# Token-mixing weights fetched earlier, their copies spread over three slots, and one pair's k squares moved to GpSimd

## The chip, the cores and the metric

One core of a Trainium2 chip. The time is that of the device for one execution, in microseconds (us); medians are of the runs that one call made. A profile is one traced execution of the kernel. "Before" is the tuned kernel, "changed" is the one under study.

## The reference, cut to what matters

```python
def _attn_ref(q, k, v, tau):                    # 8 batches, 12 heads, 448 rows, 64 wide
    q_n = q / (np.linalg.norm(q, axis=-1, keepdims=True) + 1e-06)
    k_n = k / (np.linalg.norm(k, axis=-1, keepdims=True) + 1e-06)
    scores = np.matmul(q_n, k_n.transpose(0, 1, 3, 2)) / tau
    ...                                         # softmax
    return np.matmul(attn, v).astype(np.float32)

def _moe_ref(x, w_tok1, w_tok2, w_ch1, w_ch2):  # x is the attention output, 8 x 448 x 768
    xt = x.transpose(0, 2, 1)
    h = np.maximum(xt @ w_tok1, 0.0) @ w_tok2   # token mixing: the weights of this case
    u = x + h.transpose(0, 2, 1)
    h2 = np.maximum(u @ w_ch1, 0.0) @ w_ch2     # channel mixing: most of the matmuls
    return (u + h2).astype(np.float32)
```

## The kernel before

Two heads make a pair; 48 pairs run through a loop whose pass i is called slot i here. A slot computes the scores of pair i (psS, then psX for its 64 rest rows), their exponentials on ScalarE, and the products with v of pair i-1 (psO). Token mixing follows two and three slots later: psR multiplies with w1, its relu is r, psU multiplies with w2. Once six pairs are done, channel mixing (psG, psF) fills TensorE. q and k are normalised first: squares (GpSimd and ScalarE), sums (VectorE), a logarithm and exponential on ScalarE, the scaling on GpSimd, then transposes on TensorE and a copy on VectorE, the "qk copy". The instructions of each engine run in the order in which they are written.

```python
def weights_tok():                                  # all three fetches on GpSimd's queue
    nc.gpsimd.dma_start(out=w1t[:, 0:NC, :], in_=moe_w_tok1[0:SM]...)
    nc.gpsimd.dma_start(out=w1t[0:XR, NC, :], in_=moe_w_tok1[SM:S])
    w2n.append(mix.tile([P, TT, S], FP16, name="w2n", tag="gt16", bufs=1))
    nc.gpsimd.dma_start(out=w2n[0][:], in_=moe_w_tok2...)

def place_w2():                                     # big copy, then a small one
    nc.vector.tensor_copy(out=w2t[:, :, XR:S]..., in_=w2n[0][:, :, 0:SM]...)
    nc.vector.tensor_copy(out=w2t[:, :, S:S + XR], in_=w2n[0][:, :, SM:S])
def place_w2_odd():                                 # small copy for odd batches
    nc.vector.tensor_copy(out=w2t[:, :, 0:XR], in_=w2n[0][:, :, SM:S])

def scaled(p, eng):                                 # k, then q, times their norms
    ...
        eng.tensor_tensor(out=kqs[...], in0=src, in1=_bcast_free(rn, E), op=ALU.mult)
# ... the opening, pair 0 ...
weights_tok()
cast_vx(0)                                          # GpSimd: rest rows of v
cast_v(0)                                           # VectorE: v to 16 bits
scaled(2, nc.gpsimd)
for i in range(NP_ALL + 2):
    ...
    elif 0 < i < NP_ALL:
        score(i, 0, 2 if i < 4 else 0)              # two filler matmuls ahead
        score(i, 1)
        score(i, 2)
    ...                                             # sums, norms, squares, scaling
    if i <= FIRST:
        casts()                                     # cast_v(1) in slot 3
    if i < FIRST:
        for p in tok2_at.get(i, ()):
            tok2(p)                                 # psU
        if i == 3:
            next_qk(i + 1)                          # transposes and qk copy
        if i:
            pv(i - 1)
        if i:
            score_x(i)
        if i in (0, 1, 2, 4):
            next_qk(i + 1)
        for p in tok_at.get(i, ()):
            m_tok1(p)                               # psR and r
    ...
    if i == 2:
        place_w2()
    if i == 3:
        place_w2_odd()
```

Of the kernel before, what the change touches and what calls it, by code (L numbers as in the profile page):

```python
# [22 lines left out]
def kernel(  # L23
# [12 lines left out]
    nc = tc.nc  # L36
# [100 lines left out]
    def mh(at, p):  # L137
        return at[p // HP][:, 2 * (p % HP):2 * (p % HP) + 2]

    def weights_tok():  # L140
        nc.gpsimd.dma_start(out=w1t[:, 0:NC, :], in_=moe_w_tok1[0:SM].rearrange("(p c) t -> p c t", c=NC))
        nc.gpsimd.dma_start(out=w1t[0:XR, NC, :], in_=moe_w_tok1[SM:S])
        w2n.append(mix.tile([P, TT, S], FP16, name="w2n", tag="gt16", bufs=1))
        nc.gpsimd.dma_start(out=w2n[0][:], in_=moe_w_tok2.rearrange("(tt p) s -> p tt s", p=P))

    def place_w2():
        nc.vector.tensor_copy(out=w2t[:, :, XR:S].rearrange("t a (c p) -> t a c p", c=NC),
                              in_=w2n[0][:, :, 0:SM].rearrange("t a (p c) -> t a c p", c=NC))
        nc.vector.tensor_copy(out=w2t[:, :, S:S + XR], in_=w2n[0][:, :, SM:S])  # L149

    def place_w2_odd():
        nc.vector.tensor_copy(out=w2t[:, :, 0:XR], in_=w2n[0][:, :, SM:S])

    def weights_ch1(i):
        n = C // 2
# [31 lines left out]
    def squares_x(n, eq, ek):  # L187
        square(eq, sqx[0:XR, 0:6], xh(xq, n, 6))
        square(ek, sqx[:, 6:9], xh(xk, n, HP))
# [9 lines left out]
    def rnorms(n, c0=0, c1=45):  # L199
        ssq, rn = ssqs[n % 3][:, c0:c1], rns[n % 3][:, c0:c1]  # L200
        nc.scalar.activation(out=rn, in_=ssq, func=AF.Ln, bias=tiny[:])
        nc.scalar.activation(out=rn, in_=rn, func=AF.Exp, scale=0.5)
        nc.scalar.activation(out=rn, in_=rn, func=AF.Ln, bias=eps[:])  # L203
        nc.scalar.activation(out=rn, in_=rn, func=AF.Exp, scale=-1.0)  # L204
# [242 lines left out]
    def at(slots):  # L447
        got = {}
        for p, s in slots.items():
            got.setdefault(s, []).append(p)  # L450
        return got


    FIRST = NPAIR
    early_sq = {3: 0, 4: 1, 5: 1, 6: 3, 7: 4, 8: 5, 9: 5, 10: 6, 11: 7, 12: 8, 13: 9, 14: 9, 15: 10, 16: 11, 17: 11}
    sq_slot = {p: early_sq.get(p, p - 6) for p in range(3, NP_ALL)}
    sq_at = at(sq_slot)
    sum_at = at({p: s + 1 for p, s in sq_slot.items() if p < 8 or p >= 18})

    rn_at = {}  # L460
    for n in range(1, NHALF):
        for c0, c1 in ((0, 21), (21, 45)) if n < 4 else ((0, 45),):
            s = 1 + sq_slot[3 * n + (0 if c1 == 21 else 2)]
            rn_at.setdefault(s, []).append((n, c0, c1))
    sc_at = at({p: {7: 6}.get(p, p - 2 if p < DMA_FROM else p - 3) for p in range(3, NP_ALL)})
    early_qk = {2: 0, 3: 4, 4: 6, 5: 7}
# [45 lines left out]
    with tc.manual_schedule():  # L512
# [53 lines left out]
        tpose_main(0, pst, 0)  # L566
        tpose_main(0, pst, 1)
        squares_x(0, nc.scalar, nc.gpsimd)
        rnorms(0, 21, 33)
        scaled(1, nc.gpsimd)  # L570
        nc.scalar.copy(out=qks[0][:, 0:SM], in_=pst[:, 0:SM])
# [14 lines left out]
        rnorms(0, 33, 45)  # L586
        score_rest0()
        score_x(0)
        weights_tok()
        cast_vx(0)  # L590
        cast_v(0)
        scaled(2, nc.gpsimd)
        for i in range(NP_ALL + 2):
            if i < DMA_FROM:
                loads(i)
            if DMA_FROM <= i + 2 < NP_ALL:
                dma_tpose(i + 2)
            if i - 2 in X_DMA:
                x_tpose(i - 2)
            for p in ut_at.get(i, ()):  # L600
                u_tpose(p)
            if i >= DMA_FROM:
                loads(i)

            left = next((t + 1 - i for t in sorted(tok2_at) if t >= i + (i == FIRST) and
                         any(p % NPAIR == NPAIR - 1 for p in tok2_at[t])), 6)
            if FIRST <= i < 2 * NPAIR:
                quota = max(len(queue) - 6, 0) * ns(S, DT) / (2 * NPAIR - i)
            else:
                quota = max(sum(t for t, _ in queue) - 2000.0, 0.0) / left  # L610
            def next_qk(p):
                if p < min(DMA_FROM, NP_ALL):
                    qk_copy(p, tpose(p))

            def tok2(p):
                m_tok2(p)
                if p % NPAIR == NPAIR - 1:
                    queue.extend(ch_units(p // NPAIR))

            def norm_rn():  # L620
                for n, c0, c1 in rn_at.get(i, ()):
                    rnorms(n, c0, c1)

            def next_sq(ps):
                for p in ps:
                    norm_begin(p, nc.scalar if p < 18 else nc.gpsimd, nc.scalar if p == 3 else nc.vector if p in (10, 11, 12, 15) else nc.gpsimd)

            if i == FIRST:
                next_sq([9])
                rnorms(2, 21, 33)  # L630
                norm_scale(7, nc.gpsimd)
                pv(i - 1)
                m_tok1(i - 2)
                tok2(i - 3)
                next_qk(i)
                tok2(i - 2)
                m_tok1(i - 1)
                score(i, 0)
                score(i, 1)
                score(i, 2)  # L640
                tok2(i - 1)
                norm_sums(8)
                norm_sums(9)
            elif 0 < i < NP_ALL:
                score(i, 0, 2 if i < 4 else 0)
                score(i, 1)
                score(i, 2)
            for p in sum_at.get(i, ()):
                norm_sums(p)
            if i < FIRST:  # L650
                norm_rn()

            if i < FIRST:
                next_sq([p for p in sq_at.get(i, ()) if p != 9])
                for p in sc_at.get(i, ()):
                    norm_scale(p, nc.gpsimd)
            def casts():
                for n in castx_at.get(i, ()):
                    cast_vx(n)
                for n in cast_at.get(i, ()):  # L660
                    cast_v(n)
                if i in (2, 5):
                    weights_ch1(i // 4)
                if i in (7, 8):
                    weights_ch2(i - 7)

            if i <= FIRST:
                casts()

            if i < FIRST:  # L670
                for p in tok2_at.get(i, ()):
                    tok2(p)
# [9 lines that stand above are left out]
                    m_tok1(p)  # L682
            elif i == FIRST:
                feed(0.0, 1000.0)
                score_x(i)
                feed(0.0, 1000.0)
                rnorms(2, 33, 45)
                norm_scale(8, nc.gpsimd)
                rnorms(3, 0, 21)
                next_qk(i + 1)  # L690
                next_sq(sq_at[i])
                norm_sums(10)
                feed(0.0, 1000.0)
            else:
                def norm_next():
                    norm_rn()
                    for p in sc_at.get(i, ()):
                        norm_scale(p, nc.gpsimd)

                if i >= 2 * NPAIR:  # L700
                    next_sq(sq_at.get(i, ()))
                if i < DMA_FROM:
                    norm_next()
                    casts()
                fed[0] = 0.0
                feed(quota * 0.3, 900.0 if i < DMA_FROM else 1800.0)
                if i < NP_ALL:
                    score_x(i)
                if i >= DMA_FROM:
                    norm_next()  # L710
                    casts()
                next_qk(i + 1)
                if i <= NP_ALL:
                    pv(i - 1)
                both = [p for p in tok2_at.get(i, ()) if p in tok_at.get(i, ())]
                if not both:
                    feed(quota * 0.3)
                for p in tok_at.get(i, ()):
                    m_tok1(p)
                if i < 2 * NPAIR:  # L720
                    next_sq(sq_at[i])
                if both:
                    feed(quota * 0.3, 900.0)
                for p in tok2_at.get(i, ()):
                    tok2(p)
                if i < 2 * NPAIR:
                    for p in sq_at[i]:
                        norm_sums(p)
                feed(quota * 0.4, 900.0 if i >= 2 * NPAIR else 0.0)
            if i == 2:  # L730
                place_w2()
            if i == 3:
                place_w2_odd()
        for p in ut_at.get(NP_ALL + 2, ()):
            u_tpose(p)
        feed(1e9)
# [35 lines left out]
```

## Time and profile before

| | before |
|---|---|
| median of 3 runs | 393.95 us (393.75 to 393.95) |
| span of the profiled run | 391.6 us |
| TensorE busy | 378.7 us, 97% |
| first psU starts | 27.44 us, after 1.14 us of idle TensorE |
| first psG starts | 44.54 us |

The page's lines and the waits that bound it are in the prediction below. Two more views: what GpSimd and VectorE do around the first psU. The columns are start and duration in us, engine, line, operation, output<-input, shapes and count; in brackets, the idle time before and what ended it. First GpSimd, before:

```profile
25.40 0.83 POOL L211 TENSOR_TENSOR kq<-km,rn 128x384 f16<-128x384 f32 x1 [1.41 <-ACT rn L204]
26.19 1.14 POOL L211 TENSOR_TENSOR kq<-qm,rn 128x384 f16<-128x384 f32 x1
27.29 1.17 POOL L172 CAST vx<-xv 64x192 f16<-64x192 f32 x2
```

The first two lines are the scaling of pair 4's k and q (L211), the third the cast of v's rest rows. And VectorE, before:

```profile
25.56 1.09 DVE L147 COPY w2t<-w2n 128x768 f16<-128x768 f16 x1
26.57 0.81 DVE L149 COPY w2t<-w2n 128x128 f16<-128x128 f16 x1
27.31 0.93 DVE L166 CAST vt<-vm 128x1152 f16<-128x1152 f32 x1
...
31.00 0.49 DVE L152 COPY w2t<-w2n 128x128 f16<-128x128 f16 x1
```

These are the three w2 copies (L147, L149, L152) and the cast of v's second half (L166).

### The profile page before, as it was taken

How to read it: one execution, taken by the hardware profiler on the slowest of the kernel's cores; microseconds unless marked ns; L12 is line 12 of the kernel's file. 1: busy time of each engine (PE TensorE's matmuls, PEld its weight loads, DVE VectorE, ACT ScalarE, POOL GpSimd, SP SyncE). 2: the span in 40 equal slices, each digit the busy share in tenths (PEclk: the TensorE clock that was granted, in tenths of full speed). 3: DMA queues.
4: the chain of work that ended last, by engine and by line, in shares of the span. 5: the costliest groups of instructions: out<-in, count | busy, mean ns of one | idle time of the engine just before them, and what ended most of it. 6: DMA issues, size and time to landing. Idle time of an engine off the chain costs nothing.

```text
span 391.6 us, 9075 instructions
## 1 busy us (share of the span) xinstructions
PE 378.7 (97%) x3658; PEld 228.9 (58%) x3658; DVE 193.6 (49%) x368; ACT 226.1 (58%) x411; POOL 209.6 (54%) x306
## 2 busy tenths in 40 slices
PE   7678999999999999999999999999999999999996
PEld 2356655665565656565566565565566566565554
DVE  5688758866244654446534545346434342333022
ACT  5998698843765548673775546673765535511400
POOL 4978486589476675768673938658551700000000
PEclk9699999999999999999999999999999999999999
DMA  8999989988988988999999899799982453023013
GB/s 204 267 242 221 256 238 187 201 213 241 208 170 200 211 166 194 222 166 223 199 239 174 177 253 206 155 192 175 244 142 55 133 114 69 16 60 102 3 40 121
DMA packets 137514, 67.51 MB, mean 172 GB/s; under 512 B 93248, under 2 KB 134016, under 8 KB 137472
## 3 DMA queue, kind: packets, MB, share of 16 engines
q1 hardware_dynamic: 133296, 61.36, 72.0%
q0 software_dynamic: 3632, 5.18, 7.7%
q8 instruction: 28, 0.46, 0.5%
q10 hardware_dynamic: 544, 0.39, 0.3%
q14 instruction: 14, 0.11, 0.1%
HBM read 43.38 MB, written 11.01 MB: 139 GB/s over the span
## 4 chain that ended last, share of the span: by engine, by line
PE 88%; ACT 7%; DVE 3%; DMA 1%; issue 1%; SPq 0%; DVEq 0%
PE psF L404 28%; PE psG L389 28%; PE psO L320 9%; PE psS L301 7%; PE psR L341 5%; PE psU L361 4%; ACT pt L302 3%; PE psO L322 3%; PE psX L308 2%; DMA qm<-in_q_dram 1%; PE psU L366 1%; ACT sq L178 1%; PE pst L243 1%; ACT pt L309 1%; ACT rn L203 1%
## 5 line engine op out<-in xcount | busy, mean ns | idle before, releaser
L302 ACT ACTIVATE pt<-psS 128x896 f16<-128x896 f32 x141 | 119.1, 921 | 64.6 <-PE psS L301 64.3
L389 PE MATMUL psG<-ut,wc1t 128*128 128x448 f16 x576 | 119.5, 353 | 0.2
L404 PE MATMUL psF<-wc2t,gt 128*128 128x384 f16 (+2 forms) x684 | 117.3, 323 | 0.1
L391 ACT ACTIVATE gt<-psG 128x448 f16<-128x448 f32 x96 | 51.1, 557 | 71.9 <-PE psG L389 71.9
L404 PEld LDWEIGHTS <-gt 128*128 128x128 f16 x684 | 64.5, 98 | 47.1 <-issue 6.8
L389 PEld LDWEIGHTS <-wc1t 128*128 128x128 f16 x576 | 53.2, 98 | 52.4 <-issue 8.7
L211 POOL TENSOR_TENSOR kq<-km,rn 128x384 f16<-128x384 f32 x47 | 39.4, 838 | 77.4 <-ACT rn L204 77.2
L407 DVE TENSOR_TENSOR ost<-psF,ur 128x384 f32<-128x384 f32 (+2 forms) x57 | 31.4, 550 | 87.2 <-PE psF L404 87.2
L320 PEld LDWEIGHTS <-pt 128*128 128x128 f16 x1152 | 50.8, 98 | 8.5 <-issue 2.4
L320 PE MATMUL psO<-vt,pt 128*128 128x65 f16 x1152 | 53.1, 194 | 1.1 <-ACT pt L302 0.8
L326 DVE RECIPROCAL rec<-psO 128x8 f32<-128x8 f32 x48 | 9.9, 207 | 81.5 <-PE psO L322 81.5
L193 DVE TENSOR_REDUCE ssq<-sq 128x12 f32<-128x768 f32 (+1 forms) x49 | 45.1, 929 | 6.0 <-ACT sq L178 3.1
L180 POOL TENSOR_TENSOR sq<-km 128x384 f32<-128x384 f32 x42 | 34.4, 822 | 15.1 <-DMA km<-in_k_dram 14.8
L322 PE MATMUL psO<-vx,pt 128*128 128x130 f16 x192 | 42.1, 219 | 0.0
L211 POOL TENSOR_TENSOR kq<-qm,rn 128x384 f16<-128x384 f32 x47 | 39.6, 842 | 0.0
L301 PE MATMUL psS<-qk 64*128 64x448 f16 x282 | 36.2, 357 | 1.3 <-DVE qk L261 0.9
L327 DVE TENSOR_TENSOR x<-psO,rec 128x512 f16<-128x512 f32 x48 | 33.2, 691 | 1.7
L341 PE MATMUL psR<-x,w1t 128*128 128x128 f16 x384 | 29.2, 219 | 0.1
L309 ACT ACTIVATE pt<-psX 128x448 f16<-128x448 f32 x48 | 27.1, 564 | 3.3 <-PE psX L308 2.3
L361 PE MATMUL psU<-w2t,r 128*128 128x448 f16 x96 | 25.9, 353 | 1.5 <-DVE w2t L149 1.1
L180 POOL TENSOR_TENSOR sq<-qm 128x384 f32<-128x384 f32 x30 | 24.7, 823 | 1.1 <-DVE ssq L193 0.3
L341 PEld LDWEIGHTS <-w1t 128*128 128x128 f16 x384 | 23.8, 97 | 2.1 <-issue 0.4
(76 smaller groups left out, 320.4 us busy)
## 6 DMA issues: line engine op xcount, KB each, us to landing
vm<-in_v_dram SPq DMA_DIRECT2D x16, 576.0 KB, 5.3
out_dram<-ost SPq DMA_DIRECT2D x23, 384.0 KB, 2.9
qm<-in_q_dram SPq DMA_DIRECT2D x14, 576.0 KB, 5.2
km<-in_k_dram SPq DMA_DIRECT2D x14, 576.0 KB, 5.2
wc1t<-in_moe_w_ch_dram POOLq DMA_DIRECT2D x2, 1152.0 KB, 13.9
wc2t<-in_moe_w_ch_dram POOLq DMA_DIRECT2D x2, 1152.0 KB, 12.9
out_dram<-ost SPq DMA_DIRECT2D x9, 192.0 KB, 2.7
xq<-in_q_dram SPq DMA_DIRECT2D x7, 192.0 KB, 5.1
```

The lines of the kernel that those rows point to most:

```text
L180: eng.tensor_tensor(out=out, in0=src, in1=src, op=ALU.mult)
L193: nc.vector.tensor_reduce(out=ssqs[p // HP % 3][:, lo + 6 * a0:lo + 6 * a1], in_=sq[p][:, a0:a1].rearrange("p a g e -> p (a g) e"), axis=A ...
L211: eng.tensor_tensor(out=kqs[n % 2][:, j, a, 0:NC, :].rearrange("p c (g e) -> p g c e", g=2), in0=src, in1=_bcast_free(rn, E), op=ALU.mult)
L301: nc.tensor.matmul(psS[:, g, 0:S], qk[r, P * c:P * (c + 1)], qk[r, 512:512 + S], start=True, stop=True)
L302: nc.scalar.activation(out=pt[:, 2 * S * c:2 * S * (c + 1)].rearrange("p (g s) -> p g s", g=2), in_=psS[:, :, 0:S], func=AF.Exp, scale=inv ...
L320: nc.tensor.matmul(psO[:, m, E1 * g:E1 * (g + 1)], pt[:, at:at + P], vt[:, 2 * j + g, c, 0:E1], start=(g == 0 and c == 0), stop=False)
L322: nc.tensor.matmul(psO[:, m, 0:2 * E1], pt[:, PX + P * m:PX + P * (m + 1)], vx[:, j, 0:2 * E1], start=False, stop=True)
L341: nc.tensor.matmul(psR[:, tt, :], w1t[:, m, tt * P:(tt + 1) * P], xs[p][:, m, :], start=(m == 0), stop=(m == NC))
L361: nc.tensor.matmul(psU, rs[p][:, tt, :], w2t[:, tt, lo:lo + S], start=(tt == 0), stop=by_dma and tt == TT - 1)
L389: nc.tensor.matmul(psG[:], wc1t[:, dt, ct * P:(ct + 1) * P], ut[:, dt, sp], start=(dt == 0), stop=(dt == DT - 1))
L391: nc.scalar.activation(out=gt[:, ct, sp], in_=psG[:], func=AF.Relu)
L404: nc.tensor.matmul(psF[:, 0:w], gt[:, ct, lo:lo + P], wc2t[:, ct, P * i0:P * i1], start=(ct == 0), stop=(ct == CT - 1))
```

## The change

It means to have w2 in place before the first psU. (1) The main part of w1 is fetched ahead of pair 1's scaling, where GpSimd is idle, so that w2's fetch can be issued earlier. (2) The big w2 copy moves to the end of slot 1; the small ones stay at the ends of slots 2 and 3. (3) Pair 3's k squares, and those of the rest rows, go from ScalarE to GpSimd, ahead of pair 2's scaling.

```diff
+        weights_tok1(0)                 # main part of w1, in the opening
         rnorms(0, 21, 33)
         scaled(1, nc.gpsimd)
...
-        weights_tok()
+        weights_tok2()
+        weights_tok1(1)                 # rest rows of w1
         cast_vx(0)
         cast_v(0)
+        squares_x(1, nc.scalar, nc.gpsimd)
+        squares(3, nc.scalar, nc.gpsimd)
         scaled(2, nc.gpsimd)
...
+            if i == 1:
+                place_w2()              # now the big copy alone
             if i == 2:
-                place_w2()
+                place_w2_x(S)
             if i == 3:
-                place_w2_odd()
+                place_w2_x(0)
```

More of the change, by code (lines that the diff above doesn't have):

```diff
@@ L138, in mh, with weights_tok1, weights_tok2 @@
         return at[p // HP][:, 2 * (p % HP):2 * (p % HP) + 2]
-    def weights_tok():
-        nc.gpsimd.dma_start(out=w1t[:, 0:NC, :], in_=moe_w_tok1[0:SM].rearrange("(p c) t -> p c t", c=NC))
-        nc.gpsimd.dma_start(out=w1t[0:XR, NC, :], in_=moe_w_tok1[SM:S])
+    def weights_tok1(x):
+        if x:
+            nc.gpsimd.dma_start(out=w1t[0:XR, NC, :], in_=moe_w_tok1[SM:S])
+        else:
+            nc.gpsimd.dma_start(out=w1t[:, 0:NC, :], in_=moe_w_tok1[0:SM].rearrange("(p c) t -> p c t", c=NC))
+    def weights_tok2():
         w2n.append(mix.tile([P, TT, S], FP16, name="w2n", tag="gt16", bufs=1))
@@ L148, in place_w2, with place_w2_x @@
                               in_=w2n[0][:, :, 0:SM].rearrange("t a (p c) -> t a c p", c=NC))
-        nc.vector.tensor_copy(out=w2t[:, :, S:S + XR], in_=w2n[0][:, :, SM:S])
-    def place_w2_odd():
-        nc.vector.tensor_copy(out=w2t[:, :, 0:XR], in_=w2n[0][:, :, SM:S])
+    def place_w2_x(lo):
+        nc.vector.tensor_copy(out=w2t[:, :, lo:lo + XR], in_=w2n[0][:, :, SM:S])
     def weights_ch1(i):
@@ L454 @@
     FIRST = NPAIR
-    early_sq = {3: 0, 4: 1, 5: 1, 6: 3, 7: 4, 8: 5, 9: 5, 10: 6, 11: 7, 12: 8, 13: 9, 14: 9, 15: 10, 16: 11, 17: 11}
-    sq_slot = {p: early_sq.get(p, p - 6) for p in range(3, NP_ALL)}
+    early_sq = {4: 1, 5: 1, 6: 3, 7: 4, 8: 5, 9: 5, 10: 6, 11: 7, 12: 8, 13: 9, 14: 9, 15: 10, 16: 11, 17: 11}
+    sq_slot = {p: early_sq.get(p, p - 6) for p in range(4, NP_ALL)}
     sq_at = at(sq_slot)
-    sum_at = at({p: s + 1 for p, s in sq_slot.items() if p < 8 or p >= 18})
+    sum_at = at({p: s + 1 for p, s in ({3: 0} | sq_slot).items() if p < 8 or p >= 18})
     rn_at = {}
@@ L462 @@
         for c0, c1 in ((0, 21), (21, 45)) if n < 4 else ((0, 45),):
-            s = 1 + sq_slot[3 * n + (0 if c1 == 21 else 2)]
+            s = 1 + ({3: 0} | sq_slot)[3 * n + (0 if c1 == 21 else 2)]
             rn_at.setdefault(s, []).append((n, c0, c1))
@@ L625, in next_sq @@
                 for p in ps:
-                    norm_begin(p, nc.scalar if p < 18 else nc.gpsimd, nc.scalar if p == 3 else nc.vector if p in (10, 11, 12, 15) else nc.gpsimd)
+                    norm_begin(p, nc.scalar if p < 18 else nc.gpsimd, nc.vector if p in (10, 11, 12, 15) else nc.gpsimd)
             if i == FIRST:
```

## The prediction

> **What bounds the kernel now.** I read the page's busy table first, then the 40 slices, then the waits of TensorE, and last the order of time of each engine in the first 50 us.
>
> The busy table and the slices of the kernel before:
>
> ```profile
> PE 378.7 (97%) x3658; PEld 228.9 (58%) x3658; DVE 193.6 (49%) x368; ACT 226.1 (58%) x411; POOL 209.6 (54%) x306
> ...
> PE   7678999999999999999999999999999999999996
> ...
> PEclk9699999999999999999999999999999999999999
> ```
>
> From the fifth slice on (39 us) the PE row reads 9 to the end: nothing but fewer or shorter matmuls can shorten that part, and the change touches no matmul. What the change can touch lies before 45 us. There PE is idle 391.6 - 378.7 = 12.9 us in all, most of it early. The waits of TensorE over the whole run, those over 0.5 us:
>
> ```profile
> PE pst L247 <- DVE kq L222: 1.8, 1, 1.8
> PE busy L236 <- POOL id L543: 1.4, 1, 1.4
> PE psU L361 <- DVE w2t L149: 1.1, 1, 1.1
> PE psS L301 <- DVE qk L261: 0.9, 2, 0.6
> PE psS_r L288 <- DVE qk L585: 0.8, 1, 0.8
> PE psO L320 <- ACT pt L302: 0.8, 2, 0.5
> ```
>
> The first, second and fifth end before 13.7 us, in a part whose order on PE, DVE and ACT the change leaves alone. The third is what it aims at: the first token mixing (psU) waits for VectorE to lay out w2. The chain that ended last, followed in order of time, goes through the same place:
>
> ```profile
> 16.88 2.54 ACT pt L302 x3
> ...
> 24.75 0.56 DVE qk L261
> 25.31 0.33 DVE r L344
> 25.64 1.01 DVE w2t L147
> 26.65 0.75 DVE w2t L149
> 27.40 0.04 issue
> 27.44 0.54 PE psU L361 x2
> ```
>
> The reader is to see that the two w2 copies, 1.01 + 0.75 us, stand on the chain, between the token activation r and the matmul that uses it. PE had finished the scores of slot 3 at 26.30 us and stood still until 27.44.
>
> **What the Trainium skill says.**
> - "Perfetto Trace Analysis", Identifying the Most-Contended Engine and the strategy after it: matmul busy share is a poor distance to the roofline, and a kernel may have several regimes, whose gaps are to be read within each. The trace agrees on the second point: PE is idle 1.14 us of the 1.14 us at 26.30 to 27.44 and 3.55 of the 346 us after 45.
> - "SBUF — State Buffer", Who interferes with whom: a VectorE instruction with two SBUF inputs, or a copy in a two-port mode, and a GpSimd instruction block each other, whichever starts second waiting. The trace fits: the 128x128 w2 copy took 0.81 us at 26.57 and 0.49 us at 31.00, and GpSimd's scaling beside the first took 1.14 us where it usually takes 0.83.
> - "DMA: Bandwidth & Descriptors", Issuing engines are not separate DMA queues: a transfer issued by GpSimd shares the 16 engines with those of SyncE. The trace agrees as far as it goes: from 13 us the DMA row is full and SyncE's issues stretch to 2.75 and 3.67 us; from 9 to 11 us the share is only 0.70.
> - "TensorE: Matmul & The Clock Gate", What's actually happening: the clock is granted by recent activity, half of it when cold. In this trace the granted clock is 0.50 from about 12.6 to 19.4 us and 1.00 after.
>
> **The change, part by part.** Slot i is the loop's pass i; pair numbers are those of the scores.
>
> *1. Fetching w1 earlier.* The main w1 fetch (0.74 us of GpSimd to issue) moves from 12.71 us to about 7.47 us. There GpSimd had an idle stretch of 1.45 us before pair 1's scaling at 8.91 us, which waits for ScalarE's norms. 7.47 + 0.74 = 8.21, so it hides. The fetch of w2 then starts 14.35 - 12.71 = 1.6 us earlier; it took 7.2 us to land, so I expect it about 12.7 + 7.2 = 19.9 us, where it was 21.6. The transfer moves into the stretch where the DMA share was 0.70. w1 itself is first read at 24.42 us and had landed by about 20. Direct gain: none. It frees 0.74 us of GpSimd behind 12.7 us, and makes part 2 possible.
>
> *2. w2's copies apart.* The big one (L147) goes from the end of slot 2 to the end of slot 1. VectorE there: the qk copy of pair 2 ends about 21.12; then two reductions of 0.9 until 22.92; then idle 0.89 until 23.81, when pv(1) is done. With the copy: 21.12 + 1.01 = 22.13, + 1.80 = 23.93, so the reciprocal starts about 23.95, some 0.15 us late. That delay falls on the qk copy of pair 3 (ends 25.40 for 25.23) and on r. The scores of slot 3 start at 25.41 anyway, behind two filler matmuls, so they lose about 0.05. r ends about 25.71. One small copy (0.41 to 0.75) is left before psU: 26.1 to 26.5. PE is free at about 26.35. psU so starts at 26.35 to 26.5 and not at 27.44: 0.95 to 1.1 us gained. The third copy (L152) stays where it was.
>
> *3. Pair 3's k squares on GpSimd.* ScalarE loses two instructions, at 15.69 and 16.52: 0.42 + 0.36 = 0.78 us. But the exponentials that follow start at 16.88, and the first two score matmuls of slot 1 run from 16.28 at half clock and take 0.57, so end at 16.85. ScalarE becomes free at 16.1 and waits there: the gain is 0.02 us. GpSimd gains 0.82 + 0.50 = 1.32 us of squares and has lost 0.74 of issue, so pair 2's scaling ends about 17.55 + 0.6 = 18.1; its transposes start at 19.69. The reduction of pair 3 then starts about 16.5 and ends with the rest-row sums about 18.1, ahead of the norms at 19.29. GpSimd's pairs 4 and 5 squares end about 19.8, ahead of the scaling at 20.55, which waits for ScalarE.
>
> *Does the gain last until PE is the bound?* From psU on I move everything by 1.0 and look for what holds. ScalarE: exponentials of slot 3 at 25.86 + 2.41, two squares of 0.41, then psX's exponential at about 29.1 and not 30.01. It had been idle 0.87 there, so 0.9 is all that can pass. Scores of slot 4 about 29.7 (30.61). Pair 5's scaled k and q were ready on GpSimd at 32.20 and read at 33.20; GpSimd does not move by 1.0 but loses less to the copies (0.3 us), so 31.9 against a need at 32.3: it holds. wc1's first half landed at 28.39 + 14.0 = 42.4, read at 44.54: slack 2.1. The k of half 3 landed at 27.97 + 14.6 = 42.6 and its sums were read at 45.3 after another sum: slack about 1.4. So about 0.85 us should reach the stretch that is bound by PE, and stay. **Sum**: -1.0 at psU, +0.05 at the scores, +0.1 on ScalarE, -0.02 from part 3: -0.85 us, and 393.95 - 0.85 = 393.1 us.
>
> **The rivals.**
> *A: w2 lands late.* If it came at 22 us or later, the big copy would hold VectorE's queue, and with it the sums of pairs 4 and 5, pv(1) and the scores of slot 3; the wait would only have moved. For it: DMA is full from 13 us. Against it: 7.2 us to land, as measured, ends at 19.9, some 1.2 us before the copy. It would give 393.7 to 394.2.
> *B: GpSimd becomes the bound early.* Pair 3's scaling and rest rows end at 23.99 and their transpose runs at 24.14: no slack. The big copy at 21.1 now runs beside them, and may lengthen them by 0.3 us, as the copies lengthened pair 4's scaling. That would move the qk copy of pair 3, already 0.15 late, to 0.3 late. It would leave about 0.7: 393.25.
> *C: the earlier w1 transfer delays loads of the opening.* v's first half (8.18 + 5.0 = 13.2, cast at 13.50) and k's second part (10.77 + 6.5 = 17.3, now squared at about 18.1) share the engines with it. Against: VectorE was idle 1.17 us after that cast, and the gap at 9 to 11 us has room. No change in time unless both slip by over a microsecond.
> *D: ScalarE's relief counts in full.* 0.78 us more would make 392.3, if slot 1's scores came earlier too. Nothing moves them: they wait for VectorE's qk copy, behind the transposes and the sum of pair 2, in an order left alone.
>
> **Range and chances.** The centre is 393.1. B and a slow copy cost 0.2 to 0.4, A costs all of it; D or a second wait that shrinks along (0.57 us before slot 5's scores) would add up to 0.8. The three times before lie within 0.2. I take 392.3 to 393.9. Two per cent is 7.9 us, more than half of all PE idle time, so "within 2%" is nearly sure either way.
>
> **What would show it.** In the changed kernel's waits of TensorE, psU should no longer wait for w2t, or under 0.3 us. The big w2 copy should start at 21 to 21.3 us with no idle time before it that a DMA ended; idle there proves A. The reciprocal of pv(1) should start near 23.95 us. ScalarE should be idle some 0.7 us before slot 1's exponentials, which still start near 16.87; if they start earlier, step 3 is wrong. GpSimd's scaling of pair 3 over 3.5 us proves B. Slot 4's scores should start near 29.7 us, and the first psG at about 43.7 (44.54 before). If psU starts early but psG does not, the gain was lost between them, and my walk through slots 3 to 6 is wrong. A clock that turns full elsewhere than 19.4 us would upset everything.

## More of the kernel before

The record names three different chips for the three later calls, so a kernel is compared with the kernel before of its own call.

## The result, and the profile after

The changed kernel took 393.47 us (median of 5 runs, 392.88 to 394.13), the kernel before 393.95 (5 runs). A ratio is the mean time of one kernel's runs over that of the other's of the same rounds, so not quite the ratio of the medians: 0.9989, 95% interval 0.9975 to 1.0004. The kernel was run again in two later calls: 0.9984 (0.9971 to 0.9998) and 0.9987 (0.9973 to 1.0001). Taken over all calls, 17 runs of the changed kernel have the mean 393.26 and 36 of the kernel before 393.71: 0.45 us less, with 0.31 either way (twice the standard error from the two spreads of 0.60 and 0.30). Within the three calls that ran both, the means differ by 0.42, 0.60 and 0.48. So it is faster by about half of what was predicted, and far inside two per cent.

The busy table and two rows of the slices, of the changed kernel:

```profile
PE 377.8 (97%) x3658; PEld 228.8 (58%) x3658; DVE 193.6 (49%) x368; ACT 225.4 (58%) x409; POOL 211.0 (54%) x308
...
PE   7688999999999999999999999999999999999996
...
PEclk9899999999999999999999999999999999999999
```

From the fifth slice on these two rows do not differ. Before it the busy digits hardly move; the clock row has an 8 in the second slice where it had a 6, which is chance, as the experiments show. GpSimd has 1.4 us more work and ScalarE 0.7 us less, as meant.

The waits of TensorE in the changed kernel (for whom, total us, times, longest):

```profile
PE psS L304 <- DVE qk L264: 1.6, 3, 0.9
...
PE pst L246 <- POOL kq L214: 0.3, 1, 0.3
PE psU L364 <- DVE ut L371: 0.3, 1, 0.3
PE psR L344 <- ACT pt L305: 0.3, 1, 0.3
```

The wait of psU for w2t is gone; the 0.3 us for ut is that of a later psU and was there before. In its place there are new or longer ones: the scores psS for the qk copy (1.6 us, it was 0.9), the transposes pst for GpSimd's scaling (0.3, and 0.17 at 24.50 below), psR for ScalarE (0.3). TensorE in order of time shows where they stand; L364 is the first psU, L392 the first psG:

```profile
24.50 0.23 PE L250 MATMUL pst<-id,kq 128*128 128x128 f16 x1 [0.17 <-POOL kq L225]
...
26.45 0.55 PE L364 MATMUL psU<-w2t,r 128*128 128x448 f16 x2
...
27.71 0.34 PE L246 MATMUL pst<-id,kq 128*128 128x128 f16 x3 [0.35 <-POOL kq L214]
...
30.16 0.90 PE L304 MATMUL psS<-qk 64*128 64x448 f16 x6 [0.18 <-ACT pt L312]
...
34.91 0.74 PE L304 MATMUL psS<-qk 64*128 64x448 f16 x6 [0.92 <-DVE qk L264]
...
44.44 1.30 PE L392 MATMUL psG<-ut,wc1t 128*128 128x448 f16 x6
```

and the same places before:

```profile
24.14 0.22 PE L247 MATMUL pst<-id,kq 128*128 128x128 f16 x1
...
27.44 0.54 PE L361 MATMUL psU<-w2t,r 128*128 128x448 f16 x2 [1.14 <-DVE w2t L149]
...
30.61 0.90 PE L301 MATMUL psS<-qk 64*128 64x448 f16 x6 [0.18 <-ACT pt L309]
...
35.01 1.03 PE L301 MATMUL psS<-qk 64*128 64x448 f16 x6 [0.57 <-DVE qk L261]
...
44.54 1.30 PE L389 MATMUL psG<-ut,wc1t 128*128 128x448 f16 x6
```

psU starts 0.99 us earlier, the scores of slot 4 (30.16) 0.45, those of slot 5 (34.91) 0.10 and the first psG 0.10. The scores of slot 3, which stand ahead of psU, start 0.36 us later (25.77 for 25.41). Between psU and psG nearly the whole gain was given back. GpSimd and VectorE of the changed kernel tell how:

```profile
20.68 0.82 POOL L214 TENSOR_TENSOR kq<-km,rn 128x384 f16<-128x384 f32 x1
21.47 1.14 POOL L214 TENSOR_TENSOR kq<-qm,rn 128x384 f16<-128x384 f32 x1
...
23.36 1.08 POOL L225 TENSOR_TENSOR kq<-xk,rn 64x192 f16<-64x192 f32 x2
25.42 0.83 POOL L214 TENSOR_TENSOR kq<-km,rn 128x384 f16<-128x384 f32 x1 [0.98 <-ACT rn L207]
26.21 1.45 POOL L214 TENSOR_TENSOR kq<-qm,rn 128x384 f16<-128x384 f32 x1
27.61 0.74 POOL L175 CAST vx<-xv 64x192 f16<-64x192 f32 x2
```

```profile
14.83 0.76 DVE L169 CAST vt<-vm 128x1152 f16<-128x1152 f32 x1 [0.67 <-DMA vm<-in_v_dram]
...
21.14 0.78 DVE L151 COPY w2t<-w2n 128x768 f16<-128x768 f16 x1
...
23.84 0.21 DVE L329 RECIPROCAL rec<-psO 128x8 f32<-128x8 f32 x1 [0.19 <-PE psO L325]
...
25.80 0.50 DVE L155 COPY w2t<-w2n 128x128 f16<-128x128 f16 x1
26.22 0.75 DVE L169 CAST vt<-vm 128x1152 f16<-128x1152 f32 x1
...
30.56 0.84 DVE L155 COPY w2t<-w2n 128x128 f16<-128x128 f16 x1
```

The big copy (L151, 21.14) now overlaps the scaling of pair 3 on GpSimd, whose q part takes 1.14 us where it took 0.83. The cast of v (26.22), which used to come behind two copies at 27.31, has moved up beside the q part of pair 4's scaling (26.21), which now takes 1.45 us. TensorE waits 0.35 us for it. The last small copy (30.56), beside GpSimd's scaling of pair 5 (k part at 30.52), takes 0.84 us, 0.49 before; VectorE has no pause from it up to the qk copy that slot 5's scores wait for. And in the opening VectorE and GpSimd wait for v.

### The profile page after: what moved, and what is told of

It is laid out like the page before. It is cut to its first block, busy times and chain, and to the rows that moved or that the text cites. A ratio compares the mean times of both kernels' runs of the same rounds, so it can differ in the third digit from the quotient of the medians.

```text
span 391.5 us, 9075 instructions
## 1 busy us (share of the span) xinstructions
PE 377.8 (97%) x3658; PEld 228.8 (58%) x3658; DVE 193.6 (49%) x368; ACT 225.4 (58%) x409; POOL 211.0 (54%) x308
## 4 chain that ended last, share of the span: by engine, by line
PE 87%; SPq 3%; DMA 3%; ACT 3%; DVE 2%; issue 0%; POOL 0%; ACTq 0%; DVEq 0%
PE psF L407 28%; PE psG L392 28%; PE psO L323 9%; PE psS L304 7%; PE psR L344 5%; PE psU L364 4%; PE psO L325 3%; PE psX L311 2%; DMA xk<-in_k_dram 2%; DMA km<-in_k_dram 1%; ACT pt L305 1%; SPq L124 1%; SPq L109 1%; PE psU L369 1%; PE pst L246 1%; SPq L112 1%
## 5 line engine op out<-in xcount | busy, mean ns | idle before, releaser
L392 PE MATMUL psG<-ut,wc1t 128*128 128x448 f16 x576 | 119.5, 353 | 0.2
L392 PEld LDWEIGHTS <-wc1t 128*128 128x128 f16 x576 | 53.2, 98 | 52.5 <-issue 8.7
L183 POOL TENSOR_TENSOR sq<-km 128x384 f32<-128x384 f32 x43 | 35.2, 822 | 14.7 <-DMA km<-in_k_dram 14.6
L364 PE MATMUL psU<-w2t,r 128*128 128x448 f16 x96 | 25.9, 353 | 0.3 <-DVE ut L371 0.3
## 6 DMA issues: line engine op xcount, KB each, us to landing
wc2t<-in_moe_w_ch_dram POOLq DMA_DIRECT2D x2, 1152.0 KB, 12.5
```

Source lines behind the costliest of these rows:

```text
L183: eng.tensor_tensor(out=out, in0=src, in1=src, op=ALU.mult)
L364: nc.tensor.matmul(psU, rs[p][:, tt, :], w2t[:, tt, lo:lo + S], start=(tt == 0), stop=by_dma and tt == TT - 1)
L392: nc.tensor.matmul(psG[:], wc1t[:, dt, ct * P:(ct + 1) * P], ut[:, dt, sp], start=(dt == 0), stop=(dt == DT - 1))
```

## The experiments

Twelve kernels ran, in three calls of four. The theories:

- **T**: the gain of psU is given back in slots 2 to 5, because VectorE and GpSimd hold each other up, at new places.
- **R**: the gain is there but hidden by the opening (loads that come at other times, a clock that is cold for longer).
- **S**: ScalarE's exponentials set the pace from slot 4 on, whatever precedes.

The measure that separates them is the time from the first psU to the first psG. What follows the first psG is the same in nearly every run: the device time less the start of the first psG is 348.84 to 348.90 us in 13 of the 14 profiles below (not in e4). So psG's start is the time. Here are all profiles (starts in us; "v lands" is the time from issue to landing of v's first half; "cold" is when the granted clock was half, and for how long, from the trace's clock records):

| profile | pair 0's transposes | cold clock | v lands | scores slot 2 | scores slot 3 | psU | psG | psU to psG | time |
|---|---|---|---|---|---|---|---|---|---|
| before | 8.18 | 12.6, 6.8 | 5.0 | 21.26 | 25.41 | 27.44 | 44.54 | 17.10 | 393.38 |
| changed | 8.73 | 16.1, 3.4 | 6.1 | 21.28 | 25.77 | 26.45 | 44.44 | 17.99 | 393.29 |
| e1 again | 8.34 | 12.5, 6.8 | 6.6 | 21.33 | 25.92 | 26.59 | 44.53 | 17.94 | 393.39 |
| e2 odd copy later | 8.36 | 15.4, 6.8 | 6.0 | 21.45 | 25.79 | 26.72 | 44.36 | 17.64 | 393.22 |
| e3 cast later | 8.15 | 12.7, 10.2 | 7.1 | 22.34 | 26.68 | 27.61 | 44.77 | 17.16 | 393.62 |
| e4 both | 8.47 | 13.9, 3.4 | 6.2 | 20.89 | 25.95 | 26.62 | 44.02 | 17.40 | 393.79 |
| f1 no split | 8.65 | 13.1, 6.8 | 5.3 | 21.74 | 25.88 | 27.92 | 45.01 | 17.09 | 393.86 |
| f2 no part 3 | 8.35 | 14.0, 3.4 | 6.6 | 20.68 | 25.74 | 26.41 | 44.45 | 18.04 | 393.30 |
| f3 changed, fillers | 8.46 | 22.2, 3.4 | 6.0 | 20.36 | 26.45 | 27.12 | 44.58 | 17.46 | 393.42 |
| f4 before, fillers | 8.67 | none | 5.7 | 20.95 | 25.71 | 27.75 | 44.84 | 17.09 | 393.74 |
| g1 again | 8.39 | 15.2, 6.8 | 6.4 | 21.89 | 26.11 | 27.04 | 45.10 | 18.06 | 393.94 |
| g2 w1 behind | 8.40 | 15.0, 3.4 | 4.6 | 20.52 | 25.50 | 26.17 | 44.02 | 17.85 | 392.87 |
| g3 and cast later | 8.34 | 13.7, 3.4 | 4.7 | 20.74 | 25.89 | 26.56 | 43.94 | 17.38 | 392.78 |
| g4 and odd copy later | 8.23 | 12.9, 6.8 | 4.9 | 21.39 | 25.68 | 26.46 | 43.74 | 17.28 | 392.58 |

**e1: the changed kernel again.** No edit.

> The changed kernel once more, as a control for the others of this call. Its profile so far showed psU 1.0 us earlier than before (26.45 for 27.44) but the first psG only 0.1 us earlier (44.44 for 44.54), with an opening 0.57 us late made up by a clock that was half for 3.4 us and not 6.8. Theory T (the gain is taken back in slots 3 to 5 by VectorE and GpSimd blocking each other): the first psG lies 17.9 to 18.1 us after the first psU in every profile (it was 17.10 before), whatever the opening does. Rival R (the late opening ate it): with an opening as before (pair 0's first transposes at 8.2 us) the first psG comes at 43.6 to 43.8. Time: 392.9 to 394.1, median about 393.5, and the runs with mean clock 0.996 faster by 0.4 or more than those with 0.991.

Median 393.28 (6 runs, 392.43 to 394.01), before 393.66 (11 runs), ratio 0.9984 (0.9971 to 0.9998). With an opening only 0.16 us later than that of the kernel before, and the same cold stretch, psG came at 44.53 and not at 43.6 to 43.8, and psU to psG took 17.94. That contradicts R as the main cause and agrees with T. The two runs with a mean clock of 0.995 and 0.996 average 392.86, the four with 0.991 393.29, the 0.4 expected, on few runs.

**e2: the odd copy one slot later.**

```diff
-            if i == 3:
+            if i == 4:
                 place_w2_x(0)
```

> The changed kernel with only the last small w2 copy moved from the end of slot 3 to the end of slot 4. In the changed kernel it took 0.84 us at 30.56 (0.49 before at 31.00), ending just where GpSimd's scaling of pair 5 ended its first instruction, and VectorE was then without a pause up to the qk copy of pair 5. Theory T: that copy takes 0.35 us or so of the gain; with it gone from there the scores of slot 5 start 0.3 to 0.4 us earlier against slot 4's, limited by ScalarE's exponential; total 0.3 us faster than the changed kernel. Rival R or a bound on ScalarE alone: no more than 0.1 us.

Median 392.88 (392.79 to 393.45), ratio to before 0.9981 (0.9968 to 0.9994). psU to psG fell from 17.94 to 17.64, the 0.3 us expected. In time it is 0.10 us below e1 by the means (393.04 and 393.14), which these spreads do not resolve.

**e3: the cast of v's second half behind pair 4's qk copy.**

```diff
                 for n in cast_at.get(i, ()):
-                    cast_v(n)
+                    if n != 1:
+                        cast_v(n)
...
                 if i == 3:
                     next_qk(i + 1)
+                    cast_v(1)
```

> The changed kernel with only the cast of v's second half moved behind the qk copy of pair 4 on VectorE. In the changed kernel that cast ran at 26.22, and GpSimd's scaling of pair 4's q took 1.45 us at 26.21 (usually 0.82), for which PE waited 0.35 us before pair 4's transposes. Theory T: the scaling takes 0.8 to 0.9, the 0.35 us wait goes, psX of slot 3 and slot 4's scores come 0.3 to 0.5 us earlier after psU; but the odd copy still runs into GpSimd, so the first psG moves 0.1 to 0.5. Total 0.1 to 0.5 us faster than the changed kernel. Rival R: no change beyond the spread.

Median 392.87 (392.43 to 393.62), ratio to before 0.9979 (0.9967 to 0.9991). By the means this is 0.22 us below e1, which the spreads do not resolve. Pair 4's q scaling took 0.83 us and the wait for it was gone; the odd copy took 0.18 us although it stood where it had been in the order, so that it was no longer held up:

```profile
27.47 0.83 POOL L214 TENSOR_TENSOR kq<-qm,rn 128x384 f16<-128x384 f32 x1
```

```profile
31.48 0.18 DVE L155 COPY w2t<-w2n 128x128 f16<-128x128 f16 x1
```

So this one edit removes both delays, not that of the cast alone. psU to psG was 17.16, nearly that of the kernel before. In this profile the clock was cold for 10.2 us and psU late, so GpSimd was further ahead than usual, and 17.16 flatters the edit; g3 gives 17.38 for it.

**e4: both moves.**

> Both moves together. Theory T: psU to first psG shrinks from 18.0 to 17.3 us, the time falls 0.6 to 0.8 us below the changed kernel, to about 392.8, so that the gain of 0.85 foreseen for the change appears. Rival S (ScalarE's exponentials, which run without a pause from slot 4 to 6, set the pace anyway): 0.3 us at most. Rival R: nothing.

Median 393.00 (6 runs; 392.60 to 393.79 and one of 397.04, which I cannot explain), ratio 0.9999 (0.9968 to 1.0029) because of that run. psG came at 44.02, which would make 392.87, but the profiled run took 393.79: here alone, 0.9 us was lost later. The profile shows it on VectorE and TensorE: VectorE's sums at 81.81 us waited 2.74 us for GpSimd's squares. GpSimd had waited 3.64 us for a load of v's rest rows, with the squares behind it in the queue. Then one psF, at 84.14, had to wait 0.75 us for VectorE. Before, VectorE waited 1.45 us there and TensorE not at all. So an earlier schedule has little room there, if those rows come late. The other profiles, g4's among them, do not show this wait of psF.

**f1: the split undone, the other two parts kept.**

```diff
-            if i == 1:
-                place_w2()
             if i == 2:
+                place_w2()
                 place_w2_x(S)
```

> The changed kernel with the big w2 copy put back to the end of slot 2 beside the small one; the earlier w1 fetch and pair 3's k squares on GpSimd stay. If the split is the whole source of the gain, TensorE waits 1.0 to 1.2 us for w2t before the first psU again, psU starts near 27.4, and the time is that of the kernel before within the spread (ratio 0.999 to 1.001). If the other two parts gain anything of their own, the time stays 0.3 us or more below the kernel before.

Median 393.53 (392.63 to 393.88), before 393.51 (9 runs), ratio 0.9995 (0.9982 to 1.0008). The wait of 1.14 us was back, and psU to psG was 17.09. The split is what moves psU; no gain of the other two parts shows in the time, though 0.3 us would lie within the interval.

**f2: pair 3's k squares back on ScalarE.**

```diff
-        squares_x(1, nc.scalar, nc.gpsimd)
-        squares(3, nc.scalar, nc.gpsimd)
         scaled(2, nc.gpsimd)
+        squares(3, nc.scalar, nc.scalar)
+        squares_x(1, nc.scalar, nc.scalar)
```

> The changed kernel with only pair 3's k squares back on ScalarE, in the old order. My step 3 said this part gains 0.02 us, because slot 1's exponentials wait for the scores. Then: slot 1's exponentials start within 0.1 us of where the scores let them (0.6 us after the first score matmul starts at half clock), GpSimd ends pair 3's scaling about 0.3 us earlier, the wait of TensorE of 0.17 to 0.22 us for it is gone, and psU starts 0.0 to 0.2 us earlier than in the changed kernel. Time as the changed kernel, within 0.2. If ScalarE's relief did matter, it would be 0.5 us or more slower.

Median 393.30 (393.07 to 393.98), ratio to before 0.9996 (0.9984 to 1.0009). Slot 1's exponentials started 0.60 us after its scores, without a pause behind the squares. In e4, where the squares were off ScalarE and the clock equally cold there, it was 0.60 us too, after 0.67 us of idle ScalarE. So ScalarE's relief ahead of slot 1 is idle time, as predicted. GpSimd did not profit as I expected: pair 3's scaling began at 20.64 (ScalarE's norms were ready at 20.56) where it was 20.68, and its k part took 1.14 us beside the big copy.

**f3: ten more filler matmuls in the opening of the changed kernel.**

```diff
+        busy(w, 7)
         tpose_x(0, pst)
+        busy(w, 3)
```

> The changed kernel with ten more filler matmuls on TensorE (seven ahead of pair 0's rest-row transposes, three behind), in idle stretches of 1.8 and 0.8 us. Every profile so far has one cold stretch of the granted clock of 3.4, 6.8 or 10.2 us between 12.5 and 23 us, at a place that differs from run to run. If that is what spreads the times, the fillers keep the clock full from 8 us on, the mean clock is 0.998 or more in all runs, the times lie within 0.4 of each other apart from a late load, and the median falls by 0.2 to 0.6 us. If the spread comes from the loads, the clock is full and the spread stays near 1.5 us.

Median 393.46 (392.69 to 393.76), ratio to before 0.9995 (0.9983 to 1.0008). The mean clock rose to 0.995 to 1.000, but neither the median nor, by much, the spread fell (1.07 us from lowest to highest, 1.25 to 1.76 in the three calls of the changed kernel): the three runs at 1.000 lie from 392.69 to 393.76. A miss. In this profile the cold stretch came later, at 22.2, in place of not at all. psU to psG was 17.46 and not the 17.9 that I expected of a changed kernel: slot 3 was late here, so GpSimd had finished pair 4's q scaling (25.77, 0.83 us) when the cast of v began at 26.57, while the odd copy still took 0.83 us. That fits T, since one of the two meetings fell away by chance, but it shows that psU to psG depends on the opening too.

**f4: the same fillers in the kernel before.**

> The kernel before with the same ten fillers. With the clock full in both, the two filled kernels compare the change without the clock's chance: the prediction's mechanism says the filled changed kernel is 0.3 to 0.9 us below this one, theory T (most is taken back in slots 3 to 5) says 0.1 to 0.4. In the profile psU waits 1.1 us for w2t here, and the first psG comes 17.1 us after the first psU, against 17.9 in the changed one.

Median 393.49 (393.37 to 394.37), ratio to before 1.0002 (0.9988 to 1.0015). With no cold stretch in the profile, psU still waited 1.14 us, psU to psG took 17.09, and psG came at 44.84. The opening was 0.49 us later than in the profile before, psG 0.30. By these two profiles the full clock bought about 0.2 us; TensorE now waited 2.0 us for ScalarE's exponentials, 0.8 before. The two filled kernels differ by 0.27 us in the mean, within their spread.

**g1: the changed kernel a third time.**

> The changed kernel a third time, for the mean and for one more profile. So far its two profiles give 18.67 and 18.61 us from the first score matmul of slot 3 to the first psG, and the four profiles whose second half of the w2 split is as before (the kernel before, filled or not, and the one without the split) 19.13; and 4.49 and 4.59 us from the scores of slot 2 to those of slot 3 against 4.15. I expect 18.5 to 18.7 and 4.3 to 4.6 again, v's first half landing 6 us or more after its issue (5.0 to 5.7 without the early w1 fetch), and a mean 0.3 to 0.7 us below the kernel before of this call.

Median 393.38 (6 runs, 392.18 to 393.94), before 393.67 (11 runs), ratio 0.9987 (0.9973 to 1.0001). psU to psG was 18.06, as in the two other profiles. My two narrower figures missed: slot 2's to slot 3's scores 4.22 us, slot 3's to psG 18.99. The cold stretch lasted until 22.07, so that slot 2's scores were themselves late, and the small w2 copy ahead of psU took 0.72 us and ended at 26.98: psU came 0.93 us after slot 3's scores, 0.68 and 0.67 in the two other profiles. What repeats is the time from psU on.

**g2: the early w1 fetch undone, w2 still first.**

```diff
-        weights_tok1(0)                 # in the opening
...
         weights_tok2()
+        weights_tok1(0)
         weights_tok1(1)
```

> The changed kernel with the early w1 fetch undone: GpSimd issues w2 first at 12.7 to 13.3 us, then the main part of w1, then its rest rows. If the early fetch is what delays v's first half and its rest rows (waits of 0.6 to 1.7 us on VectorE and 0.5 to 1.6 on GpSimd in the changed kernels), both waits are gone or under 0.4, the cast of v starts within 0.4 us of the copies ahead of it, and the scores of slot 1 start 0.1 to 0.4 us earlier after pair 0's first transposes. w2 still lands ahead of its copy and w1 ahead of its use, so nothing is lost: 0 to 0.4 us faster than the changed kernel. If w1 or w2 now lands late, VectorE's copy at 21 us or psR at 24.5 us waits for a DMA.

Median 393.01 (392.87 to 393.46), ratio to before 0.9984 (0.9971 to 0.9997). The waits for v were gone on both engines; v's first half landed 4.6 us after its issue, 6.4 in g1. With pair 0's transposes at the same time (8.40 and 8.39) and a full clock in both up to 15 us, slot 1's scores started at 15.79 and in g1 at 16.23: 0.44 us. That is the most that the profiles show: e2, f3 and the changed kernel's first profile, which have the early fetch and a full clock up to 15 us too, need 7.43, 7.43 and 7.48 us from pair 0's transposes to these scores, against 7.39 here and 7.84 in g1. w2 and w1 still came in time. The mean is 0.15 us below g1's, unresolved; all five runs lie within 0.6 us.

**g3: as g2, with the cast of e3.**

> Both the early w1 fetch undone and the cast of v's second half behind pair 4's qk copy. Each removes a wait of another stretch, so they should add: scores of slot 3 to first psG 18.1 us (18.6 in the changed kernel), no wait for v in the opening, first psG at 43.7 to 44.1, and 0.5 to 0.9 us below the kernel before of this call beyond what the changed kernel gains at most 0.5.

Median 392.67 (392.51 to 393.30), ratio to before 0.9976 (0.9964 to 0.9988). psU to psG 17.38, psG at 43.94. The figure from slot 3's scores to psG was 18.05, as expected.

**g4: as g3, with the odd copy of e2.**

> As the last, and the odd copy at the end of slot 4 too. With the cast late the odd copy took only 0.18 us in slot 3, so this should add nothing: within 0.2 us of the last kernel. Earlier score stretches now meet the loads near 80 us: if the rest rows of v land there after 77 us, one matmul group waits 0.7 us and takes part of the gain back.

Median 392.58 (392.29 to 392.74), ratio to before 0.9970 (0.9958 to 0.9982). psU to psG 17.28. The mean is 0.26 us below g3's; I had expected no more than 0.2, and the spreads do not settle it. GpSimd's scaling of pair 4 and VectorE's casts and last copy in this profile:

```profile
25.53 0.83 POOL L214 TENSOR_TENSOR kq<-km,rn 128x384 f16<-128x384 f32 x1 [1.18 <-ACT rn L207]
26.32 0.83 POOL L214 TENSOR_TENSOR kq<-qm,rn 128x384 f16<-128x384 f32 x1
```

```profile
13.54 0.75 DVE L169 CAST vt<-vm 128x1152 f16<-128x1152 f32 x1
...
28.34 0.90 DVE L169 CAST vt<-vm 128x1152 f16<-128x1152 f32 x1
...
34.27 0.57 DVE L155 COPY w2t<-w2n 128x128 f16<-128x128 f16 x1
```

Both halves of pair 4's scaling take 0.83 us, the cast of v's first half no longer waits for its load, and the odd copy takes 0.57 us at the end of slot 4. This is the fastest kernel here: by the means of its call it is 1.16 us below the kernel before (392.52 and 393.68) and 0.68 below the changed one (393.20).

## Why the prediction was right or wrong

The time lay in the range, and the direction was right. The size was about half of the 0.85 us predicted: 0.45 with 0.31 either way. That it came even so near is in part luck: the profiles show only some 0.1 us of the forecast gain arriving at psG, and the rest of the 0.45 is unexplained (last point).

- *What bounds.* Right. In 13 of the 14 profiles the device time is the start of the first psG plus 348.84 to 348.90 us, so all that matters happens before it. (The PE row's last digit is 6; the prediction read 9 to the end.)
- *Step 1, the w1 fetch.* Its issue did hide: it ran at 7.79 us in GpSimd's idle time, and the big copy at 21.14 found w2 landed, so rival A did not happen. But the effect of rival C was dismissed too easily, though of the two loads that it names only v's slipped in the first profile (k's second part took 6.2 us to land, 6.5 before). v's first half landed 6.0 to 7.1 us after its issue in eight of the nine profiles with the early fetch (5.3 in f1), and 4.6 to 5.7 in the five without it. g2 against g1 shows 0.44 us on slot 1's scores, other profiles under 0.1, so what it costs stays open.
- *Step 2, the copies apart.* psU was to start at 26.35 to 26.5 and started at 26.45, its wait gone. The delay of slot 3's scores was mis-sized: I gave it 0.05 us through VectorE. From slot 2's scores to slot 3's it was 4.49 and 4.59 us in the first two profiles (4.22 in the third, where slot 2 was late itself), 4.15 before. And it came not through VectorE, whose reciprocal started at 23.84 with 0.19 us to spare, but through GpSimd: pair 3's scaling ended at 24.44 and not 23.99, and its transpose waited 0.17 us. That is rival B, by the sign named for it (over 3.5 us for that scaling: 20.68 to 24.44 is 3.76).
- *Step 3, ScalarE's relief.* Right for ScalarE: in f2 and e4 the exponentials follow the scores by the same 0.60 us. Rival D is out. For GpSimd it was mis-sized: its squares ended at 20.71 us and not at 19.8, so pair 3's scaling (20.68) came straight behind them and no longer waited for ScalarE.
- *Does the gain last.* **This step failed.** It said that GpSimd "loses less to the copies (0.3 us)" and that about 0.85 us would reach psG. Instead psU to psG grew from 17.10 to 17.94, 17.99 and 18.06 us, so 0.84 to 0.96 of the 1.0 us went back. That is the sign that the prediction itself named: psU early, psG not. I had moved everything by 1.0 us without asking which VectorE instruction would now meet which GpSimd instruction. The cast of v met pair 4's scaling (1.45 us for 0.83), and the odd copy met pair 5's (0.84 us for 0.49). Moving the odd copy brings psU to psG down to 17.64 (e2); moving the cast, which frees the odd copy too, to 17.16 (e3) and 17.38 (g3). It is theory T, but not T alone.
- *ScalarE's part in it.* In the five profiles without the cast's meeting (e3, e4, f3, g3, g4) the scores of slot 4 follow those of slot 3 by the same 4.22 us, and wait 0.30 to 0.55 us for ScalarE's exponentials (0.18 before): that is ScalarE's pace. So S is out only as the limit from slot 4 on, where the edits do bring slots 4 to 6 forward; between slots 3 and 4 it holds, and a late slot 3 is passed on in full. An estimate for the first profile, against the one before: of the 0.99 us at psU, 0.37 go because slot 3's scores are 0.36 late and slot 4's follow by 4.22 at best, 0.17 because they followed by 4.39, and 0.35 to the odd copy (slot 4's to slot 5's scores 4.75 us, 4.40 before). What is left is the 0.10 seen at psG. The first share comes from step 2's mis-sized delay, rival B, which is itself a meeting of VectorE (the big copy) and GpSimd (pair 3's scaling).
- *Why the time fell at all.* Two of the changed kernel's profiles have psG 0.10 and 0.01 us earlier than before's, one 0.56 later. But the profile before was of a fast run, 393.38, for a mean of 393.71. The two differences that the profiles show between kernels add to some 0.1 us (1.0 gained up to psU, 0.9 lost after), less than the mean of 0.45 and just outside its interval of 0.15 to 0.76. Whether the rest is chance or is gained ahead of slot 2, in openings that the profiles did not catch, stays open. So does the spread: among the changed kernel's runs those with a mean clock of 0.994 and more average 392.80 us (7 runs) and those with 0.991 393.58 (10 runs), yet f3's full clock brought nothing. The kernel before shows such a split too (393.41 us in 9 runs with 0.996, 393.80 in 13 with 0.991, in the later calls), and at like clock the changed kernel is 0.61 and 0.22 us below it, so a luckier share of clocks does not account for the gain.

## What to carry to other kernels

When a wait is removed, do not move the rest of the schedule by its length as a block: list which instructions on engines that hold each other up (here VectorE and GpSimd) will now run at the same time, and look for the one that gets longer. Ask too which engine works without a pause there and passes a delay on (here ScalarE between slots 3 and 4). A fetch put into idle issue time is not free if the transfers are queued: see which load it now stands ahead of. And an effect smaller than the spread of the times can still be settled by one interval inside the trace, if that interval repeats (here psU to psG: 17.85 to 18.06 us in five of the six profiles with the split, the cast and the odd copy as in the change, 17.46 in f3), while the means alone would have needed many more runs.

## What the Trainium skill lacked or had wrong

- "SBUF — State Buffer", Who interferes with whom: the rule fits what is seen, but the page, which gives two slowdowns as ratios, gives no example of its cost for a mix of short instructions. Here GpSimd's 128x384 multiplication took 0.83 us undisturbed, 1.14 to 1.24 beside one VectorE copy and 1.45 beside a copy and a cast; VectorE's big w2 copy took 0.55 to 1.26 us by what GpSimd ran beside it, and a small one 0.18 to 0.85.
- "DMA: Bandwidth & Descriptors", Issuing engines are not separate DMA queues: it says that transfers of several queues interleave, not by how much one delays another. Here an early fetch from GpSimd's queue (192 KB in the kernel's 16-bit type) put off the landing of v's first half on SyncE's queue from 4.6 to 5.7 us after its issue to 6.0 to 7.1 in eight of nine profiles.
- "TensorE: Matmul & The Clock Gate", What's actually happening: the free-running window fits (cold stretches of 3.4, 6.8 and 10.2 us, whole multiples of its 3.4, beginning anywhere from 12.5 to 16.1 us, and at 22.2 in one filled kernel). It lacks the warning that a warmer clock may be worth nothing where another engine is waited for: f4's profile had no cold stretch before 390.8 us, and its ratio to the kernel before was 1.0002; TensorE waited for ScalarE there.
